# The order of one round of a chunked scan with a feed-forward layer beside it: state products after the chunk's products, exponents two chunks ahead, dummy products in two rounds

## The chip, the core and the metric

The kernel runs on one core of a Trainium2 chip. The metric is the time of one execution on the device in microseconds (us), the median of several runs. A profiled execution has its own time and a span, from its first to its last instruction.

## The reference

A scan with decay over 768 positions (4 batches, 8 heads, width 32, state 16) is followed by a feed-forward layer over all 3072 tokens (256 to 2048 to 256, leaky rectifier).

```python
for c in range(nc):                      # chunks of the sequence
    L = exp(cum[i] - cum[j]) * causal    # decay inside the chunk
    M = einsum('bhin,bhjn->bhij', Cc, Bc) * L
    y = einsum('bhij,bhjd->bhid', M, xc) + einsum('bhin,bhnd->bhid', Cc, state) * exp(cum[i])
    state = exp(sum(la)) * state + einsum('bhjn,bhjd->bhnd', Bc * exp(cum[-1] - cum[j]), xc)
h = x @ w_in ; g = maximum(0.01 * h, h) ; out = g @ w_out
```

## The kernel before

The scan works in `NC = 12` chunks of 64 positions. A chunk needs, in the names of the code: `scores` (16 pairs of small products of C and B into the accumulator tiles `pa` and `pb`), `decays` (two products that lay the exponents of the decay into `pd`, in the first rounds also into `h`), `decay_exp` (ScalarE takes their exponential into `lt`), `weigh` (VectorE multiplies scores and decays, the half in `pa` first, then that in `pb`), `states` (products of the weighted B with x into `pb`), `keep_state` (VectorE makes the running state `ss` of it), `passed` and `passed_exp` (the exponents of the decay since the chunk's start: a product into `pa`, and ScalarE's exponential `es`), `weigh_c` and `end_decay` (GpSimd: `cd`, which is C times `es`, and `tmp`, which is the old state times its decay), `outputs` (C times state and scores times x, in `pa` first and in `pb` last), `keep_out` (ScalarE copies the outputs out of `pa` and of `pb`) and, for the first four chunks, `low_out` (VectorE keeps the rest that the copy rounds away). `spread_c` makes the two masked copies `cm` of C.

A round of the main loop, `for c in range(2, NC + 1)`, does scores of chunk c, states and outputs of chunk c-1, and prepares chunk c+1. From `c = FIRST = 4` on, each round also does one block of the feed-forward layer for the tokens that are already there: `ffn_in` (six products into `h`, each of 512 columns, then ScalarE's `gh` and a second pass over `h`, and VectorE's `gl`) and, once two blocks wait in `queue`, `ffn_out` (six products into `o`). The weights come as 64-bit floats and are taken apart by the steps of `decode`, spread over three rounds: `dec_abs` (ScalarE), `dec_clamp`, `dec_shift`, `dec_sign`, `dec_low` (VectorE), `dec_high` (ScalarE, gives `wha`) and `dec_rest` (GpSimd, gives `wla`). `keep_warm` issues products on zeros whose result nobody reads.

The order of the work on every engine is the order in which the code is written. An instruction waits for the instructions before it on the same tile, even if they touch another part of it: a product into `pb` waits until all earlier readers of `pb` are done, and a copy out of `pa` waits for the last product that was written to `pa` before it. `o01` is the accumulator pair of the feed-forward layer; before that layer uses it, it serves the first chunk. After the scan come three more stages of the feed-forward layer, in which TensorE is always busy (from about 90 us on).

Of the kernel before, what the change touches and what calls it, by code (L numbers as in the profile page):

```python
# [10 lines left out]
F32 = mybir.dt.float32  # L11
# [4 lines left out]
ALU = mybir.AluOpType  # L16
# [33 lines left out]
def scan_ffn(ctx: ExitStack, tc: tile.TileContext, a_l, bcn_l, x_l, w_l, out_l):  # L50
# [147 lines left out]
    def dspace(c, h):  # L198
        return (pd, HB[0] if c < FIRST else pd)[h]

    def yspace(c, m):
        if c:
            return quarters[m][:, :, 3 * Q:]
        return o01.rearrange("p s (a x) -> p (s a) x", a=NH2)[:, :, m * Q:(m + 1) * Q]

    cst = open_pool(scan, "cst", side="right")
    pin = open_pool(scan, "pin", bufs=3, side="right")
# [15 lines left out]
    er = cst.tile([NE, NC * 2, CT // 2], BF16, name="er")  # L223
    parts = [cst.tile([128, 3, 2 * Q], BF16, name=f"parts{i}") for i in range(2)]
    rest = cst.tile([128, 2 * Q], F32, name="rest")
    sum1 = cst.tile([64, 2 * Q], F32, name="sum1")
    odd = cst.tile([128, 2], F32, name="odd")
    sel = cst.tile([128, NG, 2], F32, name="sel")
    dram = open_pool(scan, "dram", space=bass.MemoryType.DRAM)
# [22 lines left out]
    def keep_warm(n, space):  # L252
        for _ in range(n):
            pe.matmul(space, lhsT=idle[:, :128], rhs=idle, start=True, stop=True)  # L254
# [4 lines left out]
    def fill_slots(lo, hi, copy):  # L259
        copy(dr[:KD, lo:hi], dr[:KD, SLOTS - 1:].to_broadcast([KD, hi - lo, GB, Q]))  # L260
# [108 lines left out]
    def send_rows(lo, hi):  # L369
        for hp in range(2):  # L370
            r = ROW + 3 * hp
            sp.dma_start(
                dr[r:r + 3, slot(lo):slot(lo) + hi - lo].rearrange("p s g i -> p (s g) i"),
                sums[lo * GB:hi * GB, :, hp * Q:(hp + 1) * Q].rearrange("g p i -> p g i"),
            )
# [33 lines left out]
    def spread_c(c, hps=(0, 1)):
        if c not in cms:  # L410
            cms[c] = pw.tile([128, 2, CT], F32, name="cm")
        for hp in hps:
            act.activation(cms[c][:, hp], cs[c], AF.Copy, scale=odd[:, hp:hp + 1])

    def spread_rest(c):
        pool.tensor_scalar(  # L416
            out=cms[c][:, 1], in0=cs[c], scalar1=odd[:, 1:2], scalar2=None, op0=ALU.mult,
        )

    def scores(c):  # L420
        for b in range(NB):
# [30 lines left out]
    def keep_state(c):  # L452
        ss[c] = p3.tile([128, NB, 2, D], F32, name="ss")
        z = zspace.rearrange("p q (h d) -> p q h d", h=2)
        for hp in range(2):
            if c:
                dve.scalar_tensor_tensor(  # L457
                    out=ss[c][:, :, hp], in0=z[:, :, hp], scalar=odd[:, hp:hp + 1],
                    in1=tmps[c][:, :, hp], op0=ALU.mult, op1=ALU.add,
                )  # L460
            else:
                dve.tensor_scalar(
                    out=ss[c][:, :, hp], in0=z[:, :, hp], scalar1=odd[:, hp:hp + 1], scalar2=None,
                    op0=ALU.mult,
                )
# [18 lines left out]
    def decays(c, h):  # L484
        pe.matmul(
            dspace(c, h), lhsT=dl[:KD, c].rearrange("p h i -> p (h i)"),
            rhs=dr[:KD, slot(c), halves[h]].rearrange("p g i -> p (g i)"), start=True, stop=True,
        )

    def passed(c):  # L490
        for st in range(2):
            pe.matmul(
                espace[:, st * NH2:(st + 1) * NH2], lhsT=esel,
                rhs=er[:, c * 2:c * 2 + 2, st * Q:(st + 1) * Q], start=True, stop=True,
                skip_group_check=True,
            )

    def passed_exp(c):
        es[c] = p3.tile([128, CT], F32, name="es")
        act.activation(es[c].rearrange("p (q i) -> p q i", q=NB), espace, AF.Exp)  # L500

    def weigh_c(c):
        cds[c] = p3.tile([128, CT], F32, name="cd")
# [67 lines left out]
    sign_rows(1, 4)  # L571
    spread_c(0)
    fill_slots(0, 1, act.copy)
    fill_slots(1, 3, dve.tensor_copy)
    mask_rows(1, 4)
    send_rows(1, 4)
    send_er(1, 8)
    for h in range(2):
        decay_direct(h)
# [4 lines left out]
    for h in range(2):  # L584
        decay_exp(0, h)
    act.activation(erev, pcol, AF.Exp)
    sum_rows(1, HB[0][:, :2 * Q])
    weigh_b(0)
    send_cols(1, 8, act)
    weigh(0, 0)  # L590
    weigh(0, 1)
    dve.tensor_copy(sum1, HB[0][:64, :2 * Q])
    spread_c(1)
    spread_c(2)
    keep_warm(3, pd)
    states(0)
    outputs(0)
    keep_state(0)
    scores(1)
    passed(1)  # L600
    for h in range(2):
        decays(1, h)
    keep_out(0)
    mask_rows(4, NC)
    split(1, sum1)
    low_out(0)
    alloc_lt(1)
    passed_exp(1)
    for h in range(2):
        decay_exp(1, h)  # L610
    fetch_bc(2, "t")
    fetch_x(2)
    fetch_bc(3, "bc")
    fetch_w(0)
    fetch_bc(3, "t")
    save_sums(1)
    passed(2)
    for h in range(2):
        decays(2, h)
    weigh_b(1)  # L620
    weigh_c(1)
    end_decay(1)
    passed_exp(2)
    weigh_c(2)
    weigh(1, 0)
    weigh(1, 1)
    alloc_lt(2)
    for h in range(2):
        decay_exp(2, h)
    sign_rows(4, NC)  # L630
    fill_slots(3, 4, dve.tensor_copy)
    send_rows(4, 6)
    decode(1, 1)
    for c in range(2, NC + 1):
        f = c - FIRST
        if c < NC:
            if c >= FIRST - 1 and c + 1 < NC:
                alloc_lt(c + 1)
                decays(c + 1, 0)
                decay_exp(c + 1, 0)  # L640
            scores(c)
            states(c - 1)
        if c < NC - 1:
            weigh_b(c)
        decode(c, -1)
        if c + 1 < NC:
            passed(c + 1)
            passed_exp(c + 1)
            spread_c(c + 1, (0,) if f >= 0 else (0, 1))
            weigh_c(c + 1)  # L650
        if c < NC:
            weigh(c, 0)
            weigh(c, 1)
            keep_state(c - 1)
        if c < NC - 1:
            end_decay(c)
            if f >= 0:
                spread_rest(c + 1)
        low = ffn_in(f, 0, HB[0]) if f >= 0 else None
        if c + 1 < NC:  # L660
            if c < FIRST - 1:
                alloc_lt(c + 1)
                decays(c + 1, 0)
                decay_exp(c + 1, 0)
            decays(c + 1, 1)
            decay_exp(c + 1, 1)
        decode(c, 0)
        fetch_bc(c + 2, "b")
        fetch_w(c + 3 - FIRST, (0,))
        fetch_bc(c + 2, "c")  # L670
        outputs(c - 1)
        keep_out(c - 1)
        if low:
            low()
        low_out(c - 1)
        fetch_w(c + 3 - FIRST, (1,))
        fetch_bc(c + 2, "t")
        if c == 2:
            send_er(8, NC)
            send_cols(8, NC, sp)  # L680
        if c in (3, 6, 8):
            send_rows(*{3: (6, 9), 6: (9, 11), 8: (11, 12)}[c])
        fetch_x(c + 1)
        if len(queue) > 1:
            ffn_out(*queue.popleft())
        decode(c, 1)
    fetch_w(NFA + 2)
    scan.close()
# [244 lines left out]
```

## Time and profile before

| | us |
|---|---|
| median of 3 runs (lowest to highest) | 325.84 (325.47 to 325.9) |
| the profiled execution, its time | 323.54 |
| its span | 321.8 |
| TensorE (PE) busy, share of the span | 307.7, 96% |
| VectorE (DVE) busy | 217.2, 67% |
| ScalarE (ACT) busy | 187.7, 58% |
| GpSimd (POOL) busy | 90.0, 28% |

The shares are means over stages with different limits. The change touches only the first 90 us, and in the stage after it TensorE does not wait; whatever the scan gains or loses is therefore carried to the end.

### The profile page before, as it was taken

How to read it: one execution, taken by the hardware profiler on the slowest of the kernel's cores; microseconds unless marked ns; L12 is line 12 of the kernel's file. 1: busy time of each engine (PE TensorE's matmuls, PEld its weight loads, DVE VectorE, ACT ScalarE, POOL GpSimd, SP SyncE). 2: the span in 40 equal slices, each digit the busy share in tenths (PEclk: the TensorE clock that was granted, in tenths of full speed). 3: DMA queues.
4: the chain of work that ended last, by engine and by line, in shares of the span. 5: the costliest groups of instructions: out<-in, count | busy, mean ns of one | idle time of the engine just before them, and what ended most of it. 6: DMA issues, size and time to landing. Idle time of an engine off the chain costs nothing.

```text
span 321.8 us, 7390 instructions
## 1 busy us (share of the span) xinstructions
PE 307.7 (96%) x3026; PEld 240.2 (75%) x3027; DVE 217.2 (67%) x354; ACT 187.7 (58%) x351; POOL 90.0 (28%) x115
## 2 busy tenths in 40 slices
PE   8787899999999999999999999999999999999994
PEld 3455566666788888888778888888888888888883
DVE  6665888778789999544776566776576555665551
ACT  6765676775577766643765457644576436554451
POOL 5434667775194766921000101000000000000000
PEclk9957999999999999999999999999999999999999
DMA  6758655554232100000020000000002000000003
GB/s 189 219 163 246 200 158 177 155 166 134 72 128 66 67 1 0 0 2 0 35 98 0 0 0 3 1 0 0 2 22 108 2 0 0 0 3 0 0 1 130
DMA packets 15847, 20.52 MB, mean 64 GB/s; under 512 B 3718, under 2 KB 8646, under 8 KB 15814
## 3 DMA queue, kind: packets, MB, share of 16 engines
q1 hardware_dynamic: 15462, 19.97, 19.8%
q8 instruction: 23, 0.38, 0.5%
q10 hardware_dynamic: 352, 0.09, 0.1%
q14 instruction: 10, 0.08, 0.1%
HBM read 16.76 MB, written 3.29 MB: 62 GB/s over the span
## 4 chain that ended last, share of the span: by engine, by line
PE 78%; DVE 9%; DMA 4%; issue 3%; ACT 3%; POOL 2%; SPq 0%; ACTq 0%; POOLq 0%; DVEq 0%
PE o L152 38%; PE h L152 33%; DVE lt L435 3%; DMA raw<-w_l 3%; DVE ss L457 2%; POOL cm L416 1%; PE pb L513 1%; PE pa L427 1%; PE pa L525 1%; PE pa L254 1%; ACT es L500 1%; PE pb L525 1%; PE pb L445 1%; DMA cs<-bcn_l 1%; PE pb L427 1%
## 5 line engine op out<-in xcount | busy, mean ns | idle before, releaser
L841 ACT ACTIVATE gh<-tmp 128x512 fp32r<-128x512 f32 x48 | 30.2, 629 | 49.5 <-DVE tmp L865 46.2
L843 DVE TENSOR_TENSOR gl<-tmp,gh 128x512 fp32r<-128x512 f32 x48 | 33.3, 693 | 22.2 <-ACT tmp L842 22.2
L152 PE MATMUL o<-gh,wha 128*128 128x512 f32 x120 | 47.6, 397 | 0.0
L152 PE MATMUL o<-gl,wha 128*128 128x512 f32 x120 | 46.8, 390 | 0.0
L152 PE MATMUL o<-gh,wla 128*128 128x512 f32 x120 | 46.7, 389 | 0.0
L183 ACT ACTIVATE gh<-h 128x512 fp32r<-128x512 f32 x32 | 19.1, 597 | 21.6 <-PE h L152 21.5
L842 ACT ACTIVATE tmp<-tmp 128x512 f32<-128x512 f32 x48 | 30.4, 633 | 1.5
L186 DVE TENSOR_TENSOR gl<-h,gh 128x512 fp32r<-128x512 f32 x32 | 21.9, 685 | 13.1 <-ACT h L184 12.9
L152 PE MATMUL o<-gh,whb 128*128 128x512 f32 x72 | 28.0, 389 | 0.0
L152 PE MATMUL o<-gh,wlb 128*128 128x512 f32 x72 | 28.0, 389 | 0.0
L152 PE MATMUL o<-gl,whb 128*128 128x512 f32 x72 | 28.0, 389 | 0.0
L152 PEld LDWEIGHTS o<-gh,wha 128*128 128x128 f32 x120 | 22.5, 188 | 5.1
L152 PEld LDWEIGHTS o<-gl,wha 128*128 128x128 f32 x120 | 22.5, 188 | 4.8
L152 PEld LDWEIGHTS o<-gh,wla 128*128 128x128 f32 x120 | 22.5, 188 | 4.4
L860 DVE TENSOR_TENSOR tmp<-h,tmp 128x512 f32<-128x512 f32 x16 | 11.1, 691 | 20.8 <-PE h L152 20.8
L152 PE MATMUL h<-oph,wsh 128*128 128x512 f32 x64 | 24.9, 389 | 0.0
L152 PE MATMUL h<-oph,wsl 128*128 128x512 f32 x64 | 24.9, 389 | 0.0
L152 PE MATMUL h<-opl,wsh 128*128 128x512 f32 x64 | 24.9, 389 | 0.0
L858 ACT COPY tmp<-h 128x512 f32<-128x512 f32 x16 | 9.4, 590 | 21.0 <-PE h L152 21.0
L110 DVE TENSOR_SCALAR w<-w 128x512 f32<-128x512 f32 x16 | 12.1, 758 | 10.7 <-ACT w L107 10.4
L184 ACT ACTIVATE h<-h 128x512 f32<-128x512 f32 x32 | 19.0, 594 | 0.0
L863 DVE TENSOR_TENSOR tmp<-h,tmp 128x512 f32<-128x512 f32 x16 | 11.1, 692 | 8.7 <-PE h L152 8.6
(169 smaller groups left out, 724.3 us busy)
## 6 DMA issues: line engine op xcount, KB each, us to landing
raw<-w_l SPq DMA_DIRECT2D x32, 256.0 KB, 3.3
xs<-x_l SPq DMA_DIRECT2D x12, 256.0 KB, 3.8
out_l<-ob SPq DMA_DIRECT2D x9, 256.0 KB, 2.0
bs<-bcn_l SPq DMA_DIRECT2D x12, 128.0 KB, 3.3
cs<-bcn_l SPq DMA_DIRECT2D x12, 128.0 KB
ts<-bcn_l SPq DMA_DIRECT2D x12, 128.0 KB
out_l<-wtmp SPq DMA_DIRECT2D x3, 256.0 KB
la<-a_l SPq DMA_DIRECT2D x1, 96.0 KB
```

Of the source, the lines that this page charges most:

```text
L110: dve.tensor_scalar(out=w32(f), in0=w32(f), scalar1=MAG_MIN, scalar2=MAG_MAX, op0=ALU.max, op1=ALU.min,)
L152: pe.matmul(space, lhsT=w, rhs=x, start=start and i == 0, stop=stop and i == 2, skip_group_check=again,)
L183: act.activation(gh, hp, AF.Prelu, alpha=0.01)
L184: act.activation(hp, hp, AF.Prelu, alpha=0.01)
L186: return lambda: dve.tensor_tensor(out=gl, in0=hp, in1=gh, op=ALU.subtract)
L435: dve.tensor_tensor(out=m, in0=sspace[half].rearrange("p g a x -> p a g x"), in1=m, op=ALU.mult,)
L841: act.activation(gh, v, AF.Prelu, alpha=0.01)
L842: act.activation(v, v, AF.Prelu, alpha=0.01)
L843: return g, lambda: dve.tensor_tensor(out=gl, in0=v, in1=gh, op=ALU.subtract)
L858: act.copy(a, A)
L860: dve.tensor_tensor(out=u2, in0=B, in1=a, op=ALU.add)
L863: dve.tensor_tensor(out=u3, in0=E, in1=u2, op=ALU.add)
```

## The change

Seven edits, all before or in the main loop. (1) In a round, `states(c - 1)` stands behind `outputs(c - 1)`, and `keep_state` and `end_decay` follow later. (2) `passed` and `passed_exp` are done for chunk c+2 at the round's end instead of for chunk c+1 in its middle; for chunks 1 and 2 they use free columns of `o01`. (3) The first decays of chunk c+1 stand first in every round. (4) Both masked copies of C are made by ScalarE; GpSimd's share of them is gone. (5) The row sums of the later chunks are made and split in round 2, out of `o01`, and the copy `sum1` is gone. (6) The rows of five chunks are fetched at once instead of three and then two. (7) Dummy products: four instead of three ahead of chunk 0's outputs, eight in each of rounds 2 and 3, four in round 4.

```diff
+    early_q = o01.rearrange("p s (a x) -> p (s a) x", a=NH2)
+
+    def exspace(c):
+        return espace if c > 2 else early_q[:, :, (c + 1) * Q:(c + 2) * Q]
...
-    fill_slots(1, 3, dve.tensor_copy)
+    fill_slots(1, 4, dve.tensor_copy)
     mask_rows(1, 4)
-    send_rows(1, 4)
+    send_rows(1, 6)
...
-    sum_rows(1, HB[0][:, :2 * Q])
     weigh_b(0)
...
-    dve.tensor_copy(sum1, HB[0][:64, :2 * Q])
     spread_c(1)
     spread_c(2)
-    keep_warm(3, pd)
+    keep_warm(4, pd)
+    outputs(0)
+    scores(1)
     states(0)
-    outputs(0)
-    keep_state(0)
-    scores(1)
-    passed(1)
+    for c in (1, 2):
+        passed(c)
+    alloc_lt(1)
     for h in range(2):
         decays(1, h)
+    mask_rows(4, NC)
+    keep_state(0)
     keep_out(0)
-    mask_rows(4, NC)
-    split(1, sum1)
-    low_out(0)
-    alloc_lt(1)
     passed_exp(1)
+    passed_exp(2)
     for h in range(2):
         decay_exp(1, h)
+    low_out(0)
...
     for h in range(2):
+        decays(2, h)
         decay_exp(2, h)
+    passed(3)
+    passed_exp(3)
     sign_rows(4, NC)
-    fill_slots(3, 4, dve.tensor_copy)
-    send_rows(4, 6)
     decode(1, 1)
     for c in range(2, NC + 1):
         f = c - FIRST
+        if c + 1 < NC:
+            alloc_lt(c + 1)
+            decays(c + 1, 0)
+            decay_exp(c + 1, 0)
         if c < NC:
...
             scores(c)
-            states(c - 1)
+            weigh(c, 0)
+            weigh(c, 1)
+        decode(c, -1)
         if c < NC - 1:
             weigh_b(c)
-        decode(c, -1)
         if c + 1 < NC:
-            passed(c + 1)
-            passed_exp(c + 1)
-            spread_c(c + 1, (0,) if f >= 0 else (0, 1))
+            spread_c(c + 1)
             weigh_c(c + 1)
-        if c < NC:
-            weigh(c, 0)
-            weigh(c, 1)
-            keep_state(c - 1)
-        if c < NC - 1:
-            end_decay(c)
-            if f >= 0:
-                spread_rest(c + 1)
-        low = ffn_in(f, 0, HB[0]) if f >= 0 else None
+        if c == 2:
+            sum_rows(1, o01[:, 0, :2 * Q])
+            split(1, o01[:, 0, :2 * Q])
+        if f >= 0:
+            low = ffn_in(f, 0, HB[0])
+        else:
+            keep_warm(4, o01[:, 1])
...
         outputs(c - 1)
+        if c < NC:
+            states(c - 1)
         keep_out(c - 1)
-        if low:
+        if c + 2 < NC:
+            passed(c + 2)
+            passed_exp(c + 2)
+        if f >= 0:
             low()
+        if c < NC:
+            keep_state(c - 1)
+        if c < NC - 1:
+            end_decay(c)
         low_out(c - 1)
+        if c == 2:
+            save_sums(1)
...
         if len(queue) > 1:
             ffn_out(*queue.popleft())
+        elif f <= 0:
+            keep_warm(4, o01[:, 1])
         decode(c, 1)
```

What this does to the order of the instructions is shown at three places. The first is TensorE in round 2, from the end of chunk 2's scores to the start of chunk 1's outputs. Before (`xs`, `bnd` are states, `er`, `esel` passed, `dr`, `dl` decays, `cd`, `ss` the first half of outputs):

```order
L427 MATMUL pb<-cm,bs 64x128 x2
L445 MATMUL pb<-xs,bnd 32x64 x16
L492 LDWEIGHTS esel
L492 MATMUL pa<-er,esel 128x2x64
...
L485 LDWEIGHTS dl
L485 MATMUL pd<-dr,dl 128x512
L485 LDWEIGHTS dl
L485 MATMUL h_89<-dr,dl 128x512
L513 MATMUL pa<-cd,ss 64x64 x2
```

And of the changed kernel, where `upto`, `la` is the row sum and `idle` a dummy:

```order
L425 MATMUL pb<-cm,bs 64x128 x2
L359 MATMUL o_90<-upto,la 64x128
L258 LDWEIGHTS idle
L258 MATMUL o_90<-idle 128x512
...
L483 LDWEIGHTS dl
L483 MATMUL h_89<-dr,dl 128x512
L511 MATMUL pa<-cd,ss 64x64 x2
```

States and passed have left this place, and a row sum and four dummies into the same tile `o01` have come; VectorE's split of the row sum, which reads that tile, stands on VectorE behind both `weigh` of chunk 2.

The second place is TensorE from a later round's outputs to the next round's scores. Before, `ffn_out` follows the outputs at once:

```order
L525 MATMUL pa<-lt,xs 32x64 x16
L525 MATMUL pb<-lt,xs 32x64 x16
L152 MATMUL o_90<-gh_62,wha 128x512
...
L485 LDWEIGHTS dl
L485 MATMUL pd<-dr,dl 128x512
L427 MATMUL pa<-cm,bs 64x128 x2
```

And of the changed kernel:

```order
L523 MATMUL pa<-lt,xs 32x64 x16
L523 MATMUL pb<-lt,xs 32x64 x16
L443 MATMUL pb<-xs,bnd 32x64 x16
L490 LDWEIGHTS esel
L490 MATMUL pa<-er,esel 128x2x64
...
L152 MATMUL o_90<-gh_62,wha 128x512
```

States and passed now stand between the outputs and `ffn_out`, and passed writes the tile `pa` that the copy of the outputs reads.

The third place is ScalarE in such a round. Before, from `es` to the `dec_abs` that ends the round's chain:

```order
L500 ACTIVATE es<-pa 128x256
L413 ACTIVATE cm<-cs,odd 128x256
L183 ACTIVATE gh_62<-h_89 128x512
L184 ACTIVATE h_89<-h_89 128x512
L405 ACTIVATE lt<-pd 128x512
L133 CAST wha<-w_752 128x512
L535 COPY xf_77<-pa 128x256
L535 COPY xf_77<-pb 128x256
L107 ACTIVATE w_752<-raw 128x512
```

And of the changed kernel:

```order
L416 ACTIVATE cm<-cs,odd 128x256 x2
L183 ACTIVATE gh_62<-h_89 128x512
L184 ACTIVATE h_89<-h_89 128x512
L409 ACTIVATE lt<-pd 128x512
L133 CAST wha<-w_772 128x512
L533 COPY xf_77<-pa 128x256
L533 COPY xf_77<-pb 128x256
L498 ACTIVATE es<-pa 128x256
L107 ACTIVATE w_1051<-raw 128x512
```

The exponential `es` has moved from ahead of the feed-forward layer's passes to behind the copies of the outputs, ahead of `dec_abs`. On GpSimd a round's order was `cd`, `tmp`, `cm`, `bnd`, `wla` and is now `tmp`, `wla`, `bnd`, `cd`; on VectorE `keep_state` stood between `weigh` and `dec_sign` and now stands behind `gl`, ahead of `dec_clamp` and `dec_shift`.

## Rows read from the trace of the kernel before

**Rows 1.** Windows, one stretch: busy us of PE, PEld, DVE, ACT, POOL, then TensorE's granted clock.
```profile
18.00:20.00 2.00, 1.30 (x6) 0.32 (x4) 1.77 (x5) 2.00 (x5) 0.73 (x1) 0.50 0.33 88
```
**Rows 2.** Timeline to round 5: start, us, engine, line, operation, tiles, [idle before and releaser].
```profile
12.97 0.27 PE L492 MATMUL pa<-er,esel 24*128 24x128 bf16 x2 [0.17 <-DMA er<-sums]
...
15.96 1.04 ACT L390 COPY dl<-sign 6x1024 bf16<-6x1024 bf16 x1
...
17.73 0.43 DVE L110 TENSOR_SCALAR w<-w 128x512 f32<-128x512 f32 x1 [1.10 <-ACT w L107]
...
18.38 0.69 DVE L435 TENSOR_TENSOR lt<-pa,lt 128x512 f32<-128x512 f32 x1 [0.23 <-ACT es L500]
...
20.24 0.37 PE L513 MATMUL pb<-cd,ss 32*64 32x64 f32 x2 [0.54 <-DVE ss L457]
...
22.96 0.69 PE L427 MATMUL pa<-cm,bs 32*64 32x128 f32 x4
...
29.95 0.69 PE L427 MATMUL pa<-cm,bs 32*64 32x128 f32 x4
...
37.24 0.43 PE L427 MATMUL pa<-cm,bs 32*64 32x128 f32 x4 [1.26 <-POOL bnd L478]
```
**Rows 3.** Timeline of TensorE from round 6 into round 7.
```profile
45.60 0.50 PE L152 MATMUL h<-xh,wha 128*128 128x512 f32 x1
...
47.09 0.39 PE L485 MATMUL pd<-dr,dl 118*128 118x512 bf16 x1
...
48.04 0.27 PE L513 MATMUL pb<-cd,ss 32*64 32x64 f32 x2 [0.30 <-DVE ss L457]
...
49.44 0.50 PE L152 MATMUL o<-gh,wha 128*128 128x512 f32 x1
...
50.94 0.39 PE L485 MATMUL pd<-dr,dl 118*128 118x512 bf16 x1
...
51.88 0.45 PE L445 MATMUL pb<-xs,bnd 64*32 64x64 f32 x32
52.27 0.28 PE L492 MATMUL pa<-er,esel 24*128 24x128 bf16 x2
52.48 0.50 PE L152 MATMUL h<-xh,wha 128*128 128x512 f32 x1
```
**Rows 4.** Timeline of ScalarE in the same rounds.
```profile
47.29 0.60 ACT L183 ACTIVATE gh<-h 128x512 fp32r<-128x512 f32 x1 [0.74 <-PE h L152]
...
48.30 0.59 ACT L405 ACTIVATE lt<-pd 128x512 f32<-128x512 f32 x1
49.65 0.62 ACT L133 CAST wha<-w 128x512 fp32r<-128x512 f32 x1 [0.76 <-DVE w L127]
50.17 0.37 ACT L535 COPY xf<-pa 128x256 f32<-128x256 f32 x1
...
50.70 0.68 ACT L107 ACTIVATE w<-raw 128x512 f32<-128x512 f32 x1
...
52.65 0.39 ACT L500 ACTIVATE es<-pa 128x256 f32<-128x256 f32 x1 [0.68 <-PE pa L492]
```
**Rows 5.** Timeline of VectorE in the same rounds.
```profile
46.18 0.69 DVE L435 TENSOR_TENSOR lt<-pa,lt 128x512 f32<-128x512 f32 x1
...
47.39 0.60 DVE L457 SCALAR_TENSOR_TENSOR ss<-pb,odd,tmp 128x128 f32<-128x128 f32 x2
47.91 0.68 DVE L121 SCALAR_TENSOR_TENSOR w<-raw,w 128x512 uint32<-128x512 uint32 x1
48.62 0.99 DVE L127 SCALAR_TENSOR_TENSOR w<-raw,w 128x512 uint32<-128x512 uint32 x1
...
51.41 1.11 DVE L110 TENSOR_SCALAR w<-w 128x512 f32<-128x512 f32 x1 [1.19 <-ACT w L107]
```
**Rows 6.** Timeline of GpSimd in the same rounds.
```profile
48.13 0.94 POOL L470 TENSOR_TENSOR tmp<-ss,es 128x256 f32<-128x256 f32 x1 [1.16 <-DVE ss L457]
...
50.96 1.27 POOL L136 TENSOR_TENSOR wla<-w,wha 128x512 fp32r<-128x512 f32 x1
```

More of the change, by code (lines that the diff above doesn't have):

```diff
@@ L203, in yspace @@
             return quarters[m][:, :, 3 * Q:]
-        return o01.rearrange("p s (a x) -> p (s a) x", a=NH2)[:, :, m * Q:(m + 1) * Q]
+        return early_q[:, :, m * Q:(m + 1) * Q]
     cst = open_pool(scan, "cst", side="right")
@@ L225, in scan_ffn @@
     rest = cst.tile([128, 2 * Q], F32, name="rest")
-    sum1 = cst.tile([64, 2 * Q], F32, name="sum1")
     odd = cst.tile([128, 2], F32, name="odd")
@@ L407, in decay_exp, with spread_c @@
         )
[L409 to L412, printed above, removed]
+    def spread_c(c):
+        cms[c] = pw.tile([128, 2, CT], F32, name="cm")
+        for hp in range(2):
             act.activation(cms[c][:, hp], cs[c], AF.Copy, scale=odd[:, hp:hp + 1])
[L415 to L418, printed above, removed]
     def scores(c):
@@ L492, in passed @@
             pe.matmul(
-                espace[:, st * NH2:(st + 1) * NH2], lhsT=esel,
+                exspace(c)[:, st * NH2:(st + 1) * NH2], lhsT=esel,
                 rhs=er[:, c * 2:c * 2 + 2, st * Q:(st + 1) * Q], start=True, stop=True,
@@ L499, in passed_exp @@
         es[c] = p3.tile([128, CT], F32, name="es")
-        act.activation(es[c].rearrange("p (q i) -> p q i", q=NB), espace, AF.Exp)
+        act.activation(es[c].rearrange("p (q i) -> p q i", q=NB), exspace(c), AF.Exp)
     def weigh_c(c):
@@ L615, in scan_ffn @@
     fetch_bc(3, "t")
[L616 to L619, printed above, removed]
     weigh_b(1)
@@ L622, in scan_ffn @@
     end_decay(1)
-    passed_exp(2)
     weigh_c(2)
@@ L635, in scan_ffn @@
         f = c - FIRST
+        if c + 1 < NC:
+            alloc_lt(c + 1)
+            decays(c + 1, 0)
+            decay_exp(c + 1, 0)
         if c < NC:
[L637 to L640, printed above, removed]
             scores(c)
-            states(c - 1)
+            weigh(c, 0)
+            weigh(c, 1)
+        decode(c, -1)
         if c < NC - 1:
             weigh_b(c)
-        decode(c, -1)
         if c + 1 < NC:
-            passed(c + 1)
-            passed_exp(c + 1)
-            spread_c(c + 1, (0,) if f >= 0 else (0, 1))
+            spread_c(c + 1)
             weigh_c(c + 1)
-        if c < NC:
-            weigh(c, 0)
-            weigh(c, 1)
-            keep_state(c - 1)
-        if c < NC - 1:
-            end_decay(c)
-            if f >= 0:
-                spread_rest(c + 1)
-        low = ffn_in(f, 0, HB[0]) if f >= 0 else None
+        if c == 2:
[5 more added lines that the diff above has]
+            keep_warm(4, o01[:, 1])
         if c + 1 < NC:
[L661 to L664, printed above, removed]
             decays(c + 1, 1)
@@ L671, in scan_ffn @@
         outputs(c - 1)
+        if c < NC:
+            states(c - 1)
         keep_out(c - 1)
-        if low:
+        if c + 2 < NC:
+            passed(c + 2)
+            passed_exp(c + 2)
+        if f >= 0:
             low()
+        if c < NC:
+            keep_state(c - 1)
+        if c < NC - 1:
+            end_decay(c)
         low_out(c - 1)
+        if c == 2:
+            save_sums(1)
         fetch_w(c + 3 - FIRST, (1,))
         fetch_bc(c + 2, "t")
-        if c == 2:
+        if c == 3:
             send_er(8, NC)
```

## The prediction

> **What bounds the kernel now.** I read the chain of waits first: after 90 us it is TensorE without a pause, so only the scan can change the time, and what the scan loses arrives in full. Then I read the timeline of each engine, round by round. Two stretches differ.
>
> In the later rounds (5 to 10) a round takes 6.88 us (52.48 less 45.60, [rows 3]). TensorE waits once: the second half of the outputs starts at 48.04, when `ss` is ready. Two chains of almost the same length pass through a round. One is VectorE and ScalarE: weigh at 46.18, `ss`, sign, low [rows 5], `dec_high` at 49.65, two copies, `dec_abs` at 50.70 [rows 4], clamp at 51.41, shift, the next weigh. The other goes over TensorE's passed product and `es` at 52.65 to the same weigh. The reader should see that VectorE's clamp takes 1.11 us in a round and 0.43 at 17.73 [rows 2, 5]: it ends at 52.52, 0.29 after GpSimd's `wla` (50.96 to 52.23, [rows 6]).
>
> In rounds 2 to 4 the chain is scores, states, passed, `es`, weigh, `ss`, outputs, copy, `low_out`, next scores: scores start at 22.96, 29.95 and 37.24, so 6.99 and 7.29 us a round [rows 2]. Part of it runs at half clock: 0.50 of full speed is granted from 18 to 20 us, 1.2 instead of 2.4 GHz [rows 1].
>
> **The way into round 2.** The row fetch brings five chunks now; I leave its landing and that of the exponents at 12.97 [rows 2], where it might be up to half a us later. From there, in the new order: two pairs of passed products of 0.21 (52.27 to 52.48, [rows 3]), about 13.45. They write `o01`, so the copies of chunk 0's outputs wait for them: two copies at 0.27 (0.53 for both, [rows 4]), 14.05. Two exponentials at 0.3 (0.39 less overlap), then chunk 1's two decay exponentials at 0.5 with an end of 0.59 (48.30, [rows 4]): 15.7. Weigh of chunk 1 follows, its first half 0.69 long, to 16.4; passed of chunk 3 must wait for it, since it writes `pa`. Its `es` runs to 17.2, then the 1.04 of the row at 15.96, `dec_abs` 0.68, clamp 0.43: weigh of chunk 2 starts at 19.2 instead of 18.38.
>
> Both halves of it take 1.21 (46.18 to 47.39, [rows 5]), to 20.4. Only now can VectorE split the row sum. Its first two operations, on 128 columns, I estimate at 0.25 each, below the clamp's 0.43 on 512: 20.9. The four dummies write the tile that it reads and stand ahead of the outputs on TensorE, so TensorE does nothing for some 2 us, and then dummies. A product of 512 columns costs 0.25 (1.50 for six, 49.44 to 50.94, [rows 3]), at half clock twice that: 1.0 to 2.0 us, and a decay product behind them. Outputs start at 22.2 or 23.2, before at 20.24. At 18 to 20 TensorE was busy 1.30 of 2 us and had half the clock [rows 1]; it does less now, so I take 23.2: **+3.0**.
>
> From there to the next scores took 2.72 (20.24 to 22.96). Now states (0.39, [rows 3]), a copy of `pb` that waits for them (0.38), and `ss` (0.60, [rows 5]) come between outputs and `low_out`: +1.4, of which I give back 0.4 for the clock that returns during the unbroken work: **+1.0**. Scores of chunk 3 start at 27.0 instead of 22.96.
>
> **Round 3.** Here the order gains. At full clock: scores with the half in `pb` 0.3 late, 1.0; both weighs 1.35 with the wait; outputs 1.40 (48.04 to 49.44), states 0.39, copy 0.40, `ss` 0.65, `low_out` 0.4: 5.6 instead of 6.99, **-1.4**. The eight dummies lie under weigh and under copy and `ss` and cost nothing; if the clock fell they would cost their 1.0 each four. Scores of chunk 4: 32.55 instead of 29.95.
>
> **Round 4** is the first with `wla` and with decode steps, and GpSimd's order matters. `tmp` and `wla` now follow each other directly behind `ss`, just when VectorE has clamp and shift. The rows show how such pairs meet: `tmp`, issued at 48.13 during `dec_sign` (to 48.59), ended 0.48 after that; `dec_low`, issued at 48.62 during `tmp` (to 49.07), took 0.99 and ended 0.54 after it [rows 5, 6]. They alternate, each waiting for the other. So clamp waits for `tmp`, `wla` for clamp, and shift for all of `wla` (1.27): 1.1 us more ahead of weigh. A gain of about 1.0 from the shorter chain and the 1.1 cancel: **+0.05**. Without the meeting it would be -0.9.
>
> **Rounds 5 to 10.** The wait for `ss` ahead of the outputs goes: 48.04 less 47.5 (47.09, a decay product of 0.32 and two products of the outputs), 0.5 us a round. But passed now waits for the copy out of `pa`, and that copy stands on ScalarE behind `gh`, the second pass, a decay exponential and `dec_high`. That closes a chain of its own: copy 0.37, passed 0.25, `ffn_out` 1.50, decays and scores 0.94 (50.94 to 51.88), `ffn_in` 1.49 (45.60 to 47.09), 0.20 to `gh`, 1.01 from `gh` to the decay exponential, 0.49 to `dec_high`, 0.52 to the copy: 6.78 [rows 3, 4]. This is the floor; the 0.5 cannot be had.
>
> The other chain, from the start k of the copy: passed k+0.42, `es` 0.38 later (52.27 to 52.65), `dec_abs` k+1.09, clamp 0.71 later (50.70 to 51.41), k+1.80. The copy of `pb` ends at k+0.65, `ss` k+1.30, `tmp` from k+1.44 to k+2.06 at a length estimated at 0.62 (0.94 less the wait). Clamp waits for it and ends at k+2.4, `wla` runs to k+3.67, shift ends 0.29 later, weigh starts at k+3.98. From weigh to the next copy: 1.21, sign 0.71 (47.91 to 48.62), low as long where nothing meets it, `dec_high` 0.55: 3.2. Together 7.2, against 6.88. I take 7.2, as the longer of the two: +0.32 for five rounds, **+1.6**. Bounds: -0.5 by the floor, and by clamp falling behind `wla` (below) +4.6.
>
> The masked copy that moves to ScalarE adds about 0.45 there, in a stretch where ScalarE waits 0.74 for `h` [rows 4]: nothing, if that cover is gone 0.45. At the end (chunks 10 and 11) there is no passed left and `ss` is out of the chain: **-0.4**. The dropped `sum1` copy, the single row fetch and the fill for it lie beside the exponents' transfer and cost nothing; a late landing would show in full, up to 0.5.
>
> **Sum.** 3.0 + 1.0 - 1.4 + 0.05 + 1.6 - 0.4 = +3.85. On the profile's 323.54 that is 327.4. The runs' median, 325.84, lies 2.3 higher; on it the forecast is **329.7**.
>
> **The rivals.** *B, the rounds at their floor:* the clock stays at 2.4 GHz into round 2 (outputs at 22.2, and the rest of that round shorter: -1.35), and clamp and shift slip past GpSimd (-0.9 and -0.5 instead of +1.6). All together 3.85 - 1.35 - 0.95 - 2.1 = -0.55; one or two of the three give +0.5 to +2.5, around 327.3. For it: the dummies, which fill every other gap of these rounds. Against: the 2 us without any work ahead of them, after which the kernel before had half the clock [rows 1], and the alternation in [rows 5, 6].
>
> *C, `wla` ahead of clamp:* if clamp is issued 0.26 later than I work out, `tmp` has ended and `wla` runs; clamp then ends at k+3.65, `bnd` slips in, shift ends at k+4.5: 0.6 more a round, +3.0, 332.7. Of this meeting the rows show that the later one waits (clamp 1.11 behind `wla`), not yet which wins when both wait. The Trainium skill ("SBUF — State Buffer", Who interferes with whom) says that VectorE's two-port operations and GpSimd share ports, that whoever issues first holds them for its whole instruction and that the other blocks; by it the sum stays 329.7 with clamp issued first and is 332.7 with `wla` first, and the 1.11 agrees.
>
> *D, faster:* the copies of the outputs reach ScalarE before states are done, because `dec_high` is ready earlier than its place in the queue suggests. Passed then waits for nothing, and a round is what TensorE has to do, 6.88 less 0.53: -3.2 over six rounds, and -0.9 in round 4: 3.85 - 1.6 - 3.2 - 0.95 = -1.9, 323.9. It needs copies 0.5 us earlier; it decides once a round falls below 6.5. Against it is the queue: the copy's end comes 2.6 us after `ffn_in` (0.20, 1.01, 0.49, 0.52 and 0.37, as in the floor), while states are done after 2.1 (a decay product 0.32, outputs 1.40, states 0.39).
>
> **How the numbers follow.** My case 0.57 (328 to 331.5), B 0.20 (faster, same and slower in 0.02, 0.08 and 0.10), C 0.06, D 0.17 (faster 0.13, same 0.04). About 0.2% can be told from no change here, so 325.2 to 326.5 counts as the same. Faster 0.15, same 0.12, slower 0.73. The range leaves out most of D and half of C: 325.5 to 331.8.
>
> **What would show it.** Dummies of round 2 starting near 20.9, at half clock; scores of chunks 3, 4 and 5 near 27.0, 32.5 and 39.9; in later rounds passed waiting for the copy, weigh every 7.1 to 7.3, shift as long as `wla`. Wrong: chunk 5's scores before 38, or weighs less than 6.8 apart.

## The result and the profile after

| | before | after |
|---|---|---|
| median of 4 runs each on one chip (lowest to highest), us | 325.87 (325.47 to 326.07) | 328.57 (327.93 to 328.61) |
| ratio, 95% interval | | 1.008 (1.0062 to 1.0097) |
| the profiled execution, us | 323.54 | 328.61 |
| its span, us | 321.8 | 326.9 |

The change makes the kernel slower by 2.7 us. The two profiles differ by 5.1; why these are not the same number is the first question of the experiments.

First the windows of TensorE on the way into round 2, after (columns as in [rows 1]; the granted clock is the third number from the right):

```profile
18.00:20.00 2.00, 2.00 (x35) 1.05 (x34) 0.06 (x1) 1.95 (x4) 0.85 (x2) 0.50 0.81 278
20.00:22.00 2.00, 0.18 (x1) 0.10 (x1) 1.84 (x5) 1.37 (x4) 0.00 (x0) 0.50 0.00 0
...
24.00:26.00 2.00, 2.00 (x66) 1.36 (x65) 0.00 (x0) 0.60 (x1) 0.00 (x0) 0.50 0.58 190
26.00:28.00 2.00, 1.84 (x94) 1.31 (x75) 0.52 (x2) 1.05 (x3) 0.00 (x0) 0.98 0.93 305
```

Half clock (0.50, 1.2 GHz) lasts until 26, through a window in which TensorE works 0.18 of 2 us; from 28 on the clock is full. Next the timeline to round 5, which answers to [rows 2]:

```profile
14.13 0.38 PE L490 MATMUL o<-er,esel 24*128 24x128 bf16 x4 [2.46 <-DMA er<-sums]
...
20.47 0.69 DVE L433 TENSOR_TENSOR lt<-pa,lt 128x512 f32<-128x512 f32 x1
...
21.97 0.28 DVE L365 TENSOR_TENSOR rest<-o,parts 64x128 f32<-64x128 f32 x1
...
22.31 0.58 PE L258 MATMUL o<-idle 128*128 128x512 bf16 x1 [2.13 <-DVE rest L365]
23.11 1.06 PE L258 MATMUL o<-idle 128*128 128x512 bf16 x2 [0.22 <-issue]
...
24.53 0.37 PE L511 MATMUL pa<-cd,ss 32*64 32x64 f32 x2
...
28.47 0.43 PE L425 MATMUL pa<-cm,bs 32*64 32x128 f32 x4
...
34.17 0.43 PE L425 MATMUL pa<-cm,bs 32*64 32x128 f32 x4
...
41.29 0.43 PE L425 MATMUL pa<-cm,bs 32*64 32x128 f32 x4
```

The exponents land 1.16 later than before (14.13 against 12.97). The dummies wait 2.13 for VectorE's split and run at half clock; outputs of chunk 1 follow at 24.53, scores of chunks 3, 4 and 5 at 28.47, 34.17 and 41.29. Last a later round, all engines, which answers to [rows 3 to 6]:

```profile
59.32 0.69 DVE L127 SCALAR_TENSOR_TENSOR w<-raw,w 128x512 uint32<-128x512 uint32 x1
...
60.20 0.61 ACT L133 CAST wha<-w 128x512 fp32r<-128x512 f32 x1
...
60.71 0.38 ACT L533 COPY xf<-pa 128x256 f32<-128x256 f32 x1
...
61.14 0.27 PE L490 MATMUL pa<-er,esel 24*128 24x128 bf16 x2 [0.50 <-ACT xf L533]
...
62.22 0.62 POOL L468 TENSOR_TENSOR tmp<-ss,es 128x256 f32<-128x256 f32 x1 [3.55 <-DVE ss L455]
...
62.47 0.65 DVE L110 TENSOR_SCALAR w<-w 128x512 f32<-128x512 f32 x1 [0.40 <-ACT w L107]
...
62.80 1.46 POOL L136 TENSOR_TENSOR wla<-w,wha 128x512 fp32r<-128x512 f32 x1
...
63.16 1.38 DVE L115 TENSOR_SCALAR w<-w 128x512 uint32<-128x512 uint32 x1
...
63.77 0.50 PE L152 MATMUL h<-xh,wha 128*128 128x512 f32 x1
...
64.31 0.50 PE L152 MATMUL h<-xh,wla 128*128 128x512 f32 x1
...
64.46 0.68 DVE L433 TENSOR_TENSOR lt<-pa,lt 128x512 f32<-128x512 f32 x1
```

Passed waits 0.50 for the copy. `tmp` goes first, clamp ends 0.28 after it, `wla` follows clamp, shift ends 0.28 after `wla`: the alternation foreseen. The second product of `ffn_in` stands at 64.31, 0.05 after `wla` ends (64.26). Weigh starts 7.05 after the weigh of the round before (57.41); from round to round it is 7.05 to 7.10, where it was 6.88 [rows 3].

### The profile page after: what moved, and what is told of

Read it like the earlier page. It is cut to its first block, busy times and chain, and to the rows that moved or that the text cites. A ratio compares the mean times of both kernels' runs of the same rounds, so it can differ in the third digit from the quotient of the medians.

```text
span 326.9 us, 7433 instructions
## 1 busy us (share of the span) xinstructions
PE 309.0 (95%) x3043; PEld 239.7 (73%) x3048; DVE 218.6 (67%) x352; ACT 189.8 (58%) x358; POOL 79.4 (24%) x108
## 4 chain that ended last, share of the span: by engine, by line
PE 81%; ACT 8%; DVE 4%; DMA 2%; POOL 2%; issue 2%; SPq 0%; POOLq 0%; DVEq 0%; ACTq 0%
PE o L152 38%; PE h L152 36%; POOL wla L136 2%; ACT lt L409 1%; DMA er<-sums 1%; ACT gh L183 1%; ACT h L184 1%; ACT wha L133 1%; DVE ss L455 1%; DMA sums<-parts 1%; PE pa L258 1%; PE o L258 1%; PE pa L425 1%; ACT xf L533 1%; PE pa L511 1%
## 5 line engine op out<-in xcount | busy, mean ns | idle before, releaser
L152 PE MATMUL h<-xh,wla 128*128 128x512 f32 x40 | 16.5, 413 | 2.0 <-POOL wla L136 1.8
```

The source lines that it names most:

```text
L152: pe.matmul(space, lhsT=w, rhs=x, start=start and i == 0, stop=stop and i == 2, skip_group_check=again,)
```

## The experiments

Twelve runs were made, all profiled. Each is compared with the kernel before on its own chip, whose medians went from 324.89 to 325.64, so the ratios are the safer column. The last four columns are read from each kernel's profiled execution: `er`, the start of the first passed product behind the exponents' landing, the starts of the scores of chunks 3 and 5, and the length of a later round.

| kernel | median | ratio to before (95%) | er | scores 3 | scores 5 | round |
|---|---|---|---|---|---|---|
| before, first profile | 325.87 | | 12.97 | 22.96 | 37.24 | 6.88 |
| after | 328.57 | 1.008 (1.0062 to 1.0097) | 14.13 | 28.47 | 41.29 | 7.07 |
| before again | 325.53 | 0.9983 (0.9955 to 1.0012) | 12.67 | 23.13 | 39.07 | 6.88 |
| before with dummies | 323.66 | 0.9952 (0.9919 to 0.9985) | 13.00 | 23.12 | 36.06 | 6.88 |
| after without dummies | 329.3 | 1.0128 (1.0093 to 1.0163) | 14.07 | 26.66 | 42.41 | 7.07 |
| rows three first | 327.47 | 1.0052 (1.0034 to 1.007) | 13.10 | 27.55 | 40.38 | 7.06 |
| no first dummies | 328.72 | 1.009 (1.0056 to 1.0124) | 13.54 | 27.18 | 40.55 | 7.06 |
| dummies ahead of the split | 326.85 | 1.0043 (1.0023 to 1.0064) | 13.73 | 26.43 | 39.24 | 7.07 |
| `wla` early | 325.44 | 1.001 (0.9977 to 1.0044) | 13.71 | 27.88 | 40.03 | 6.77 |
| exponential ahead of `dec_abs` | 330.81 | 1.0179 (1.0142 to 1.0217) | 13.00 | 27.52 | 41.04 | 7.47 |
| exponential behind `dec_abs` | 328.19 | 1.0095 (1.0066 to 1.0124) | 13.24 | 28.01 | 40.67 | 6.89 |
| three edits, first try | 324.9 | 0.9994 (0.9976 to 1.0012) | 12.63 | 26.70 | 39.01 | 6.93 |
| rows, dummies, `wla` | 322.34 | 0.9919 (0.9892 to 0.9946) | 12.94 | 24.18 | 36.32 | 6.76 |
| best: these and the exponential | 321.47 | 0.99 (0.9863 to 0.9937) | 12.53 | 25.11 | 37.11 | 6.30 |

### What the kernel before does between its executions

> The kernel before, unchanged, profiled a second time. The profile of the changed kernel lies 5.1 us above that of the kernel before (328.61 against 323.54), the medians only 2.7. If the earlier profiled execution of the kernel before was an unusually quick one, this one comes out nearer to 325.9 and the 2.3 us show as one or two places where a landing or the clock differs, most likely in the first 30 us (scores of chunk 3 later than 22.96). If instead a profiled execution of this kernel is always quicker than its other runs, it comes out at 323.5 again, with scores of chunk 3 at 22.96.

Measured: 326.1 for the profiled execution, a span of 324.1, and 323.57 to 326.94 over ten runs. The first theory holds in this: 323.54 is the quick end of a wide range. The place it named first is wrong (scores of chunk 3 came at 23.13); the time is lost in rounds 3 and 4. The windows of this second profile of before:

```profile
24.00:26.00 2.00, 2.00 (x63) 0.98 (x47) 0.00 (x0) 0.27 (x1) 0.00 (x0) 0.50 0.71 235
...
34.00:36.00 2.00, 2.00 (x6) 1.19 (x5) 2.00 (x5) 0.11 (x1) 0.83 (x2) 0.50 0.27 89
```

It stays at half clock up to 36, and from the weigh of chunk 2 to that of chunk 5 its rounds take 7.59, 7.59 and 7.40. The first profile had full clock from 24 to 26 and again after 32, with half clock between (0.50 at 28 to 30), and took 7.03, 6.91 and 6.98:

```profile
24.00:26.00 2.00, 1.23 (x55) 0.57 (x41) 0.58 (x1) 1.00 (x3) 0.54 (x1) 1.00 0.83 245
```

Over all runs the mean granted clock tells the same: six executions of before with 0.983 took 323.49 to 323.66, those with 0.963 to 0.968 took 325.1 to 327.03, and most lie between.

### The dummies by themselves

The kernel before with the changed kernel's twenty dummies of rounds 2 to 4 and nothing else:

```diff
         low = ffn_in(f, 0, HB[0]) if f >= 0 else None
+        if f < 0:
+            keep_warm(4, o01[:, 1])
...
             ffn_out(*queue.popleft())
+        elif f <= 0:
+            keep_warm(4, o01[:, 1])
```

> The kernel before with dummies alone added: four in rounds 2 and 3 at the place of the changed kernel's (behind states and passed, ahead of the outputs), and four at the end of rounds 2, 3 and 4. Two profiles of the kernel before differ by 2.3 us (321.8 and 324.1), and nearly all of it comes between the scores of chunk 3 (22.96, 23.13) and of chunk 5 (37.24, 39.07): in the quicker one the granted clock was back at 1.00 from 24 to 26 and again after 31, in the slower one it was 0.50 up to 36. Theory: dummies are worth having by themselves, the clock comes back near 26 in every execution, and the kernel before comes to 323.0 to 324 with a narrow spread, so that the change's order costs more than the 2.7 us that the medians show. Rival: in this order TensorE has no idle time to fill, the dummies only put off outputs and ffn_out by 1.0 to 2.0 a round: 326.5 to 328.

Measured: 323.66, and full clock from 22 on:

```profile
20.00:22.00 2.00, 2.00 (x98) 1.49 (x98) 1.40 (x3) 1.36 (x3) 1.76 (x2) 0.81 0.89 279
22.00:24.00 2.00, 2.00 (x70) 1.05 (x69) 0.75 (x2) 1.01 (x3) 0.00 (x0) 1.00 0.90 232
```

The theory's time holds; its narrow spread does not (321.86 to 325.91). The other half of the table, the changed kernel without its dummies in these rounds:

```diff
-        else:
-            keep_warm(4, o01[:, 1])
...
-        elif f <= 0:
-            keep_warm(4, o01[:, 1])
```

> The changed kernel without the dummies of rounds 2, 3 and 4 (twenty products whose result is read by nobody; the four ahead of chunk 0's outputs stay). With the kernel before alone (325.6), the kernel before with dummies (323.7) and the changed kernel with dummies (328.6) it completes a table of order against dummies. Theory: the dummies are worth about as much in this order as in the other, about 2, by the clock alone: 330 to 331, the granted clock at 0.50 until some 36, rounds 3 and 4 at 6.5 to 7.6 as in the slower profile of before, and a wider spread. Rival: the changed order leaves fewer gaps from round 3 on and brings the clock back by itself, as it did by 29 without the first four; without the wait for the split it gains what the dummies held up: 327 to 328.6.

Measured: 329.3, half clock up to 40, and 8.68 from the weigh of chunk 4 to that of chunk 5:

```profile
38.00:40.00 2.00, 2.00 (x68) 1.45 (x69) 1.02 (x2) 1.88 (x4) 0.00 (x0) 0.50 0.26 53
40.00:42.00 2.00, 1.44 (x83) 0.95 (x67) 0.58 (x3) 1.65 (x5) 0.00 (x0) 0.97 0.85 283
```

The time lies between the two forecasts, 0.7 below the theory's and 0.7 above the rival's, and the wider spread did not come (328.69 to 329.7); the clock decides against the rival, for the order does not bring it back by itself. By the ratios, on 325.6: the dummies give 0.48% or 1.6 us in either order (1 to 0.9952; 1.0128 to 1.008), and the order costs 1.28% or 4.2 us with or without them. Order stands here for all edits but these dummies, the longer row fetch included. So the 2.7 of the result are some +4.2 and some -1.6; each carries an uncertainty of 1.1 to 1.3 from the intervals.

### The landing of the exponents

```diff
-    fill_slots(1, 4, dve.tensor_copy)
+    fill_slots(1, 3, dve.tensor_copy)
...
-    send_rows(1, 6)
+    send_rows(1, 4)
...
     sign_rows(4, NC)
+    fill_slots(3, 4, dve.tensor_copy)
+    send_rows(4, 6)
```

> The changed kernel with its rows fetched three chunks first and then two, as before. In the changed kernel the exponents er land at 14.13 instead of 12.97. Theory: the longer fetch did that; then passed starts at about 13.0, weigh of chunk 1 at 15.7 instead of 16.77, outputs of chunk 1 and scores of chunk 3 about 1.1 earlier, the rounds unchanged at 7.07: 327.4. Rival: the landing varies by itself from execution to execution, or the second fetch in round 2 costs as much again: no change, 328.6, and passed between 12.9 and 14.2 without order.

Measured: passed at 13.10, scores of chunk 3 0.92 earlier than after, rounds unchanged, 327.47, which is 1.1 less by the medians and 0.9 by the ratios. The theory holds. The fill of the slots, which the edit also shortens (0.69 instead of 1.75), is not what delayed the landing: it ends before the row fetch is issued, at 8.99 in both kernels. Over all profiles the five-chunk fetch gives starts between 13.00 and 14.13 (seven, mean 13.63), the three-chunk fetch between 12.53 and 13.10 (seven, mean 12.83): so some 0.8 of the 1.16 comes from the fetch, and the rest is spread.

### The dummies that wait for the split

```diff
-        else:
+        elif c > 2:
             keep_warm(4, o01[:, 1])
```

> The changed kernel without the four dummies ahead of the outputs in round 2 (a dummy's result is read by nobody). Theory: they wait for VectorE's split (22.31) and then run at half clock; without them the outputs of chunk 1 start when ss is ready, about 21.3 instead of some 24.3, and scores of chunk 3 at 26.5 instead of 28.47, the rounds unchanged: 326.6, with half the clock up to some 26 as before. Rival: the dummies bring the clock back; without them it stays at half through round 3, which is then 1 to 2 us longer: 328 to 329.

Measured: 328.72, no gain. From scores of chunk 2 to those of chunk 3 it takes 9.42 instead of 10.07, then half clock lasts until nearly 30 (0.58 at 28 to 30) and round 3 takes 6.25 instead of 5.70. Theory and rival each had half. Next come the same dummies, moved ahead of the row sum:

```diff
+        if f >= 0:
+            low = ffn_in(f, 0, HB[0])
+        else:
+            keep_warm(4, o01[:, 1])
         if c == 2:
             sum_rows(1, o01[:, 0, :2 * Q])
             split(1, o01[:, 0, :2 * Q])
-        if f >= 0:
-            low = ffn_in(f, 0, HB[0])
-        else:
-            keep_warm(4, o01[:, 1])
```

> The changed kernel with the four dummies of round 2 ahead of the row sum on TensorE instead of behind it, so that they no longer wait for VectorE's split. Leaving them out did not help: scores of chunk 3 came 0.65 earlier measured from those of chunk 2, but the granted clock stayed at 0.50 until about 29 and round 3 took 6.25 instead of 5.70. Theory: both the wait and the half clock cost; with the dummies run while TensorE waits for weigh (19 to 22), outputs of chunk 1 start when ss and lt are ready, and the clock is back by 26 or earlier: -0.6 to -1.2, 327.4 to 328. Rival: the 2 us without work in front of the outputs come back behind these dummies, the clock stays at half until 29, and nothing is gained: 328.6.

Its timeline of TensorE:

```profile
19.09 1.89 PE L258 MATMUL o<-idle 128*128 128x512 bf16 x4
20.91 0.69 PE L359 MATMUL o<-upto,la 128*64 128x128 f32 x2
21.53 0.61 PE L483 MATMUL h<-dr,dl 118*128 118x512 bf16 x1
22.07 0.37 PE L511 MATMUL pa<-cd,ss 32*64 32x64 f32 x2
...
24.53 0.34 PE L443 MATMUL pb<-xs,bnd 64*32 64x64 f32 x13 [0.69 <-issue]
```

TensorE goes from the dummies to the outputs without a gap, the clock is back by 24 (0.92 at 22 to 24), and scores of chunk 3 follow those of chunk 2 after 8.43: 1.64 less than after. In time it is 326.85, less than after by 1.7 (medians) or 1.2 (ratios), of which 0.4 is an earlier landing of the exponents (13.73). Against no dummies here (9.42) the four cost 0.65 behind the split and save 1.0 ahead of it. Both differences are too small: among the state products the run without them pauses 0.46 and this one 0.69, which the changed kernel does not; without these pauses, to which the last section comes back, I estimate 1.1 and 1.2.

### What sets the 7.07 of a later round

`wla`, made at the end of the round before, ahead of `tmp`:

```diff
             weigh(c, 1)
-        decode(c, -1)
...
             keep_state(c - 1)
+            decode(c + 1, -1)
         if c < NC - 1:
             end_decay(c)
```

> The changed kernel with GpSimd's wla made ahead of tmp, at the end of the round before. Theory: clamp and shift of a round are long because tmp and wla come just beside them; with wla done sooner, clamp and shift take about 0.45 each, and a round is the chain over passed and the copy, 6.78 to 6.9 instead of 7.07: about -0.2 to -0.3 in each of seven rounds, 326.5 to 327.2. Rival: the round's length is already set by the chain over passed, and clamp and shift have room: rounds stay at 7.07, 328.6. Third: tmp now waits behind wla, bnd with it, and states are late: rounds of 7.3, 330.

Measured: rounds of 6.77 and 325.44, 3.1 less than after by the medians and 2.3 by the ratios, more than expected. The same stretch as above, in this kernel:

```profile
58.59 1.28 POOL L136 TENSOR_TENSOR wla<-w,wha 128x512 fp32r<-128x512 f32 x1 [3.18 <-ACT wha L133]
...
60.85 0.73 DVE L115 TENSOR_SCALAR w<-w 128x512 uint32<-128x512 uint32 x1
...
61.47 0.50 PE L152 MATMUL h<-xh,wha 128*128 128x512 f32 x1
...
61.61 0.69 DVE L433 TENSOR_TENSOR lt<-pa,lt 128x512 f32<-128x512 f32 x1
61.81 0.40 PE L152 MATMUL h<-xh,wla 128*128 128x512 f32 x1
```

`wla` takes 1.28 instead of 1.46, shift 0.73 instead of 1.38, and `ffn_in`'s second product follows the first after 0.34 instead of 0.54. Both my chains became shorter here, so this alone does not say which one held the 7.07. Two edits of ScalarE's queue tell more. The first puts a decay exponential behind the copies, ahead of `dec_abs`:

```diff
             decays(c + 1, 1)
-            decay_exp(c + 1, 1)
...
             passed_exp(c + 2)
+        if c + 1 < NC:
+            decay_exp(c + 1, 1)
```

> The changed kernel with the second decay exponential of a round moved on ScalarE from ahead of dec_high and the copies of the outputs to behind them. With wla moved alone the rounds came to 6.77, the 6.78 that I had worked out as the floor. Theory: the floor is the chain copy, passed, ffn_out, scores, ffn_in, gh, exponential, dec_high, copy; an exponential less on it is 0.47 less, and rounds come to about 6.5 (wla, which follows the copies through ss and tmp, still ends late): 7 rounds by -0.5 = -3.5, 325.1. Rival: the chain over weigh, sign, low and dec_high (worked out at 7.2 before, slack of only 0.14 ahead of dec_high in the trace) holds the round, and it gains at most 0.14: 327.6 or no change. Third: the exponential, now behind es, holds up dec_abs and with it clamp, shift and weigh: rounds of 7.2 or more, 329.5.

Measured: rounds of 7.47, 330.81. The third case came true. In this kernel `dec_high` waits for VectorE, and clamp meets GpSimd's `wla` the other way round:

```profile
53.53 0.62 ACT L133 CAST wha<-w 128x512 fp32r<-128x512 f32 x1 [1.00 <-DVE w L127]
...
56.13 1.27 POOL L136 TENSOR_TENSOR wla<-w,wha 128x512 fp32r<-128x512 f32 x1
56.29 1.39 DVE L110 TENSOR_SCALAR w<-w 128x512 f32<-128x512 f32 x1 [0.89 <-ACT w L107]
...
57.72 0.73 DVE L115 TENSOR_SCALAR w<-w 128x512 uint32<-128x512 uint32 x1
```

The second puts it behind `dec_abs`, and the first decays behind the scores so that `pd` is free in time; `wla` stays where it was:

```diff
+        if c < NC:
+            scores(c)
         if c + 1 < NC:
             alloc_lt(c + 1)
             decays(c + 1, 0)
             decay_exp(c + 1, 0)
         if c < NC:
-            scores(c)
...
-            decay_exp(c + 1, 1)
...
         decode(c, 1)
+        if c + 1 < NC:
+            decay_exp(c + 1, 1)
```

> The changed kernel with only the exponential's edit of the best version: the second decay exponential behind dec_abs, the first decays behind the scores; wla stays where it was, and clamp and shift still meet tmp and wla. It tells which of the two chains holds the changed kernel's 7.07. Theory: the chain over the copy, 6.78 and 0.3 of waiting for wla, holds it, but the chain over weigh, sign, low and dec_high is only some 0.13 shorter (low ends at 60.01 and dec_high starts at 60.20): rounds of 6.9 to 7.0, dec_high waiting for low, -0.5 to -1.0, 327.6 to 328.1. Rival: the chain over weigh has more room than that: rounds of 6.6, 325.4. Second rival: the chain over weigh holds the 7.07 alone: nothing changes, 328.6.

Measured: rounds of 6.89, and `dec_high` now waits for `dec_low`:

```profile
59.15 0.62 ACT L133 CAST wha<-w 128x512 fp32r<-128x512 f32 x1 [0.23 <-DVE w L127]
...
60.09 0.27 PE L490 MATMUL pa<-er,esel 24*128 24x128 bf16 x2 [0.34 <-ACT xf L533]
```

With 0.47 taken from the copy's chain the round falls by 0.18 and then hangs on the other chain. So in the changed kernel the copy's chain is the longer one, 7.07, and the chain over weigh and `dec_low` follows, at 6.89 as this run has it. In time (328.19, and a ratio whose interval covers the 1.008 of after) the 0.18 a round can't be told; in the profile it takes 49.32 from the scores of chunk 5 to the last outputs of the scan, instead of 50.31.

### Towards a version that beats both

Rows three first, `wla` early and the exponential ahead of `dec_abs`:

> The changed kernel with three edits: rows fetched three chunks first (measured alone -1.1), wla at the end of the round before (alone -3.1), and the second decay exponential behind the copies. Theory: rounds of 6.3 to 6.4, which is what TensorE has to do in a round (6.77 less its 0.51 of waiting for the copy): 328.6 - 1.1 - 3.1 - 7 by 0.4 = 321.6, below both kernels. Rival: with the copy's chain shorter, the chain over weigh, sign, low and dec_high (weigh to copy 3.3, copy to weigh 3.2) becomes the longer one and rounds stay at 6.5 to 6.7: 322.9 to 324.

Measured: 324.9 and rounds of 6.93, more than the rival allowed, but by the chain that it named: `dec_high` waits 0.57 for `dec_low`. With the copy's chain shortened, the exponential ahead of `dec_abs` lies on the other one. The next two leave that out:

> The changed kernel with the rows fetched three first (-1.1 alone), the dummies of round 2 ahead of the row sum (-1.7 alone, of which some 0.4 is an earlier landing of er) and wla at the end of the round before (-3.1 alone). Theory: the three act in different places and add up: 328.6 - 1.1 - 1.5 - 3.1 = 322.9, rounds at 6.77, scores of chunk 3 at 25.5 to 26. Rival: what is won ahead of round 2 is lost again at a transfer that arrives at a fixed time, or to half the clock: 324 or more.

> The changed kernel with the rows fetched three first, the dummies of round 2 ahead of the row sum, wla at the end of the round before, the second decay exponential behind dec_abs (not ahead of it, where it cost 0.47 a round on the chain over clamp and weigh), and the first decays behind the scores again. Theory: two chains of nearly the same length pass through a round, one over copy, passed, ffn_out and ffn_in (6.78 with wla out of the way), one over dec_abs, clamp, shift, weigh, sign, low and dec_high (6.93 with the exponential ahead of dec_abs, so about 6.46 without it); only an edit that shortens both gains. This one takes an exponential, 0.47, from the first and adds nothing to the second: rounds of 6.4 to 6.5, 321 to 322. Rival: the exponential now holds up the products of the next round (pd comes free later) or the second weigh, and rounds stay at 6.75 or above: 323.2 or more.

Measured: 322.34 and 321.47, ratios of 0.9919 and 0.99, both below the kernel before and far below the changed one. In the first of them the edits add up (322.9 was the sum). The two ratios can't be told apart; the profiles can: in the last one TensorE is busy 13.85 of the 14 us from 52 to 66, and a round takes 6.24 to 6.39 instead of 6.76. Both profiles also lose time in rounds 4 to 6, on which more below.

## Why the prediction came out as it did

**Direction and size.** Slower was right, 328.57 lies in the range, and the sum of +3.85 stands against +2.7 in the medians. Step by step, from the profiles:

| step | forecast | measured | from |
|---|---|---|---|
| way into round 2 | +3.0 | +4.3 | outputs 24.53 less 20.24 |
| outputs to scores of chunk 3 | +1.0 | +1.2 | 3.94 less 2.72 |
| round 3 | -1.4 | -1.3 | 5.70 less 6.99 |
| round 4 | +0.05 | -0.2 | 7.12 less 7.29 |
| rounds 5 to 10 | +1.6 | +0.9 | 5 by 0.19 |
| end | -0.4 | +0.2 | last outputs 91.60 less 86.44, less the steps above |

**The way in** missed at one term: I left the landing at 12.97, and it came 1.16 later. Counted from there the chain was right to 0.3: weigh of chunk 2 at 20.47 (19.2 plus 1.16 is 20.36), split, dummies at 22.31 (20.9 plus 1.16 is 22.06), at half clock. That the wait for the split, not the dummies' work, is their price is shown by moving them: scores of chunk 3 then come 1.64 sooner after those of chunk 2. Of the 1.16, some 0.8 is the five-chunk fetch, which I had put beside the transfer at no cost, with half a us at most.

**Round 3 and round 4** are right in size (for round 4 my two terms give +0.1, not +0.05); the alternation in round 4 is in the trace, and `wla` early takes it away (round 4 to 6.45, scores of chunks 4 and 5 at 33.58 and 40.03).

**Rounds 5 to 10**: 7.07 where I gave 7.2, but my reason, "as the longer of the two", took the wrong chain. I charged the meeting with GpSimd to shift and weigh alone. It also delays `wla`, and `ffn_in`'s second product waits for that: it starts 0.20 later behind the first and takes 0.50 instead of 0.40, so the copy's chain, worked out at 6.78, becomes 7.07. The other one is 6.89; my 7.2 for it was too long mainly from the copy to weigh, 3.98 where the trace has 3.75 (60.71 to 64.46). The floor itself was right: 6.77 with `wla` out of the way. The Trainium skill ("SBUF — State Buffer", Who interferes with whom) says that issue order decides who blocks; both orders are in these runs. With `tmp` first, clamp 0.65 and shift 1.38; with `wla` issued 0.16 ahead of clamp, clamp 1.39 and shift 0.73, which is rival C's meeting, and it came when `dec_abs` was put off by half a us; rounds were then 0.40 longer, where C had 0.6.

**The end** lost instead of gaining. Weigh of chunk 11 does come sooner behind that of chunk 10 (5.68 instead of 6.14), but the `ffn_in` of that round then waits for `wla`, the same dependency that I had not counted:

```profile
85.53 0.50 PE L152 MATMUL h<-xh,wla 128*128 128x512 f32 x1 [1.01 <-POOL wla L136]
```

**The clock** is the step that failed most, though it does not show in the total. The dummies stood in my sum as a cost alone, and I added the 2.3 by which the median exceeds the profiled execution of before as if it were the same for any kernel. It is half clock in rounds 2 to 4 of before, of which most of its executions have more than the first profile (0.983 of full speed over the whole span, the highest of any of its runs), and which the dummies shorten (0.989 to 0.995 in the kernel before with dummies). In the profiles the sum should have been +5.1, and in the medians +4.2 for the order and -1.6 for the dummies. That my +3.85 came within 1.2 of the medians' +2.7 is in part luck: the landing that I left out (+1.2 in this profile) takes back half of the 2.3 that I carried over.

**Rival B** asked for full clock in round 2; it came at 26 only. The half clock in [rows 1], which I set against B, stands beside 1.30 of 2 us of work and not behind 2 us without any; the changed kernel has that case, 0.18 of 2 us and then 0.50 up to 26. **Rival D** did not come: the copy is held by ScalarE's queue, as argued, and only taking an exponential out of that queue, together with `wla` early, gave rounds of 6.3.

## What to carry to other kernels

Where two chains of nearly equal length pass through a round, work out both, follow every late result to all its readers, and judge an edit by what it takes from both: here each edit alone gave 0.2 to 0.3 a round, and an exponential moved one place too early cost 0.4. Four dummies that waited for another engine gained nothing here, and moving the same four ahead of that wait took 1.2 to 1.7 us off; the gain of dummies is priced against the clock that most executions have, not against the one that was profiled. Where TensorE stops among like products, count its instructions. Look at the spread of the runs before adding a difference between median and profile to a forecast.

## What the runs showed that was not expected

Most of the variants meet pauses of TensorE for which the profile names no releaser, in the middle of a group of like products. The longest are in the one with rows, dummies and `wla` (profiled at 324.75, its slowest run), 0.96 ahead of half the scores of chunk 5 and 1.52 between the tenth and the eleventh state product, and in the best one, 1.43:

```profile
38.01 0.32 PE L425 MATMUL pa<-cm,bs 32*64 32x128 f32 x2 [0.96 <-issue]
...
43.39 0.42 PE L443 MATMUL pb<-xs,bnd 64*32 64x64 f32 x22 [1.52 <-issue]
```

```profile
39.33 0.32 PE L425 MATMUL pa<-cm,bs 32*64 32x128 f32 x2 [1.43 <-issue]
```

After the last one the granted clock falls to 0.50 for 40 to 42, and the rounds from chunk 4 to chunk 6 take 7.72 and 7.93 instead of the 6.3 of later rounds, so up to some 3 us hang on it (an estimate). Dummies aside, the traces have twelve such pauses of over 0.25 up to 96 us, in eight of the runs; the changed kernel, which reaches this part of the program later, shows none.

By the traces TensorE waits for its instructions there. They come over a queue of their own, in blocks of 16384 bytes:

```profile
q8 instruction: 24, 0.39, 0.5%
```

The run with rows, dummies and `wla` moves 24 such blocks for 6117 recorded instructions of TensorE, so a block holds some 256. In every kernel the pauses lie at the same counts, whatever product stands there: in the first 50 us 348, 475, 730, and 858 or 859 weight loads are ahead of them, steps of about 128 or twice that, and a product goes with each weight load, so the steps are 256 instructions or twice that. In each of the twelve TensorE goes on 1.34 to 1.56 after the end of such a block, and at no block's boundary in any of the fourteen profiles sooner than 1.20. This is read from the traces and was not tested by an edit, and why the blocks come late just there stays open. The Trainium skill ("Runtime: NRT & Kernel Launch", Terms) says that each engine's instruction memory is refilled in blocks of 16 KiB; the 16384 bytes of these traces agree.
